# Zero matmuls in TensorE's waits and three loads spread out, at the head of a fused attention and FFN kernel

## The chip, the cores and the metric

The kernel runs on one core of a Trainium2 chip. The metric is the device time in microseconds (us) of one execution, taken as the median of several runs. The five engines of the core work side by side, each through its own queue in order: TensorE (PE in the profile, with its weight loads as PEld), VectorE (DVE), ScalarE (ACT), GpSimd (POOL) and SyncE (SP), which here issues most of the DMA transfers.

## The reference, cut to what matters

One transformer block on x of 2048 rows and 1024 columns in bf16: 32 heads of 32 columns that share one K and one V, and a gated FFN of 3584 columns.

```
h  = x + A(layernorm(x))
h2 = h + B(layernorm(h))

A(x): q = x @ wq              (32 heads of 32)
      k = x @ wk; v = x @ wv  (one head, shared)
      p = softmax(q k^T / sqrt(32))
      return (p v) @ wo
B(x): return (sigmoid(x @ w_gate) * (x @ w_up)) @ w_down
```

## The kernel before

**Units of work.** The rows of x are 16 tiles of 128. The attention runs in *bursts*: a burst is eight (later four) score matmuls on TensorE (`s_burst`, line 706, matmuls at 725 and 715) and two exponentials of 128x1024 on ScalarE (`one_exp`, line 748). The scores have six PSUM banks, and burst k waits on TensorE until all exponentials but one of the bursts before it are done. All other matmuls fill the time between bursts: projections, PV, the output projection and the FFN. They run as *groups* (`_Group`, `run_group`, `run_item`), each in one of the two banks of `X_ps`, and each ends with an eviction on VectorE or ScalarE. Groups of the kind "f" are those that go through `mm_list`, with the matmul of line 327.

**The head.** Up to the 25th burst the order is written out by hand (lines 1412 to 1532), with the strings of `HEAD` for the pieces between bursts. Layernorm of a tile is `ln1_stats` (VectorE, line 411, with GpSimd for the power), `ln1_sub` and `ln1_mult`. The tile is then transposed to `xnT`: tiles 0 and 1 on TensorE, tiles 2 to 15 by a DMA transpose that SP issues (`transposed`, line 533). Groups in the head:
- u0 to u7: a query projection for one of the first eight units of the attention, 16 matmuls of 128 columns; u7 and u4 read the last quarter of wq.
- K0 to K7: the keys of two tiles, 8 matmuls of 256 columns, evicted by ScalarE at line 556. K1 needs tiles 2 and 3, K2 tiles 4 and 5, K3 tiles 6 and 7.
- V0 to V7: the values of two tiles, 16 matmuls of 32 columns.

The order around the change is: burst 2, burst 3, u5, K1, burst 4, V1 and u6, burst 5, burst 6, K2, burst 7, V2, u7, u4, burst 8, a projection of 8 matmuls of 256 columns, burst 9, K3, V3. ScalarE's order is written out too: the eviction of K1 stands between the two exponentials of burst 3, that of K2 between those of burst 6, and that of K3 between those of burst 9.

**The planner.** While the program is written, the kernel keeps a clock of its own for each engine (`k_pe`, `k_act`, `k_dve`, `k_sp`, and `k_dma` for the transfers) and adds a written duration for each instruction. `when(...)` is the latest of the times at which ticks of semaphores fall by these clocks, plus 0.05; `need(engine, ...)` moves the engine's clock there and emits the waits. `mode(...)` adds 0.104 where TensorE changes the kind of its matmuls. A DMA transpose takes 1.3 of SP's clock, then 1.2 of the transfers' clock, and lands 2.0 later; a load takes its size by 275 KB per us of the transfers' clock, and lands 2.2 later. In the head the clocks do not choose an order. In the main loop (from line 1561) they do: a burst goes out when its due time has come by `k_pe`, otherwise a group's next item.

**Loads.** x comes in tiles of 256 KB. Tiles 0 to 7 are issued at the start. The others are issued by `ln1_out` (line 449) on SP's queue behind the transpose of the tile that `LOADS` names, as is "q3", the last quarter of wq, 512 KB.

**Zeros.** `zeros` (line 462) runs matmuls of 128 columns on an operand of zeros, whose result nobody reads: 64 at the start, 8 between the transposes of tiles 0 and 1, and 4 at some places of `HEAD` ("z").

Of the kernel before, what the change touches and what calls it, by code (L numbers as in the profile page):

```python
# [12 lines left out]
P = 128  # L13
# [39 lines left out]
def when(*ticks):  # L53

    return max([0.0] + [t[0].time(t[1]) + 0.05 for t in ticks if t is not None])


def need(eng, *ticks):
    clk = CLK[id(eng)]
    for t in ticks:  # L60
        if t is not None and t[0].emit is not None and t[1] > t[0].n:
            t[0].emit(t[1])
    clk[0] = max(clk[0], when(*ticks))
    for t in ticks:
        if t is not None:
            t[0].wait(eng, t[1])
# [18 lines left out]
def bass_sequential_preLN__grouped_kv_mqa__glu_gated_glu__prompt_kernel(  # L85
# [37 lines left out]
    G_SUM, NPB = 3, 4  # L123
    HG = 3
    HEAD = ['u', 'Vu', 'L', '', 'VULu', 'u', 'VPP', 'wL', 'LzPULz', 'zPLz', 'W', 'LzP', 'PPzL', 'VVL', 'PPV', '', 'UPP', 'UP', 'PV', 'U', 'PU', '', '', '']
    HEAD_U = [5, 6, 7, 4]
    ORDER = [(0, 0), (0, 1), (0, 2), (1, 0), (0, 3), (1, 1), (1, 2), (1, 3)]
    ORDER += [(t_, i_) for t_ in range(2, NT) for i_ in range(NQ // 2)]
# [10 lines left out]
    with ExitStack() as es:  # L139
# [31 lines left out]
        X_ps = EC(nc.psum_tensor("X_ps", [P, 2, 512], F32))  # L171

        k_pe, k_dve, k_act, k_pool, k_sp, k_dma = [0.0], [0.0], [0.0], [0.0], [0.0], [0.0]
# [4 lines left out]
        def ctr(name, clk=None):  # L178
            return _Ctr(EC(nc.semaphore(name)), clk)

        c_pe, c_dve, c_act = ctr("c_pe", k_pe), ctr("c_dve", k_dve), ctr("c_act", k_act)
        c_pool, c_s, c_e, c_pv = ctr("c_pool", k_pool), ctr("c_s", k_pe), ctr("c_e", k_act), ctr("c_pv", k_pe)
# [29 lines left out]
        def xn(t):  # L212
            return xn2[:, t % 4, :] if t % 4 < 2 else hn[:, t % 4 - 2, :]
# [25 lines left out]
        def _(unused):  # L239
            sp, pe, act, dve, pool = nc.sync, nc.tensor, nc.scalar, nc.vector, nc.gpsimd  # L240
# [34 lines left out]
            warm = pairs[:, 1, 0:256]  # L275
# [11 lines left out]
            bank_free = [None, None]  # L287
            pe_mode = [None]

            def mode(m):  # L290
                if pe_mode[0] != m:
                    k_pe[0] += T_SW
                    pe_mode[0] = m

            def bank_time(b):
                f = bank_free[b]
                return 1e9 if f == "open" else f(False) if callable(f) else when(f)

            def open_group(g):
                b = min((bank_time(b), b) for b in range(2) if bank_free[b] != "open")[1]  # L300
                g.bank = b
                f = bank_free[b]
                need(pe, f(True) if callable(f) else f)
                bank_free[b] = "open"

            main = [False]
# [5 lines left out]
            def by_columns(g):  # L312
                if not main[0]:
                    return False
                while issued and issued[0] < k_pe[0] - I_US:
                    issued.popleft()
                if 4 * len(issued) > I_MAX and g.items[0][0] < 0.2:
                    return False
                more = busy(pv[0]) or pv_follow[0] is not None
                if pe_mode[0] == "pv":  # L320
                    return more or k[0] < NB
                n = pv_next[0]
                return pe_mode[0] == "s" and (more or n < NQC * NQ and k[0] >= min(BPG * (n + 1) + 1, NB - (n == NQC * NQ - 1)))

            def mm(out, lhsT, rhs, start, stop):
# [4 lines left out]
                                    stop=stop, tile_position=(0, DH * j), skip_group_check=True)  # L330
                return ins

            def run_item(g):
                if g.bank is None:
                    need(pe, *[v() if callable(v) else v for v in g.after])
                    open_group(g)
                mode("pv" if g.kind == "f" and by_columns(g) else g.kind)
                issued.extend([k_pe[0]] * (2 if pe_mode[0] == "pv" else 0))
                part[0] = (part[0] + 1) % 2 if pe_mode[0] != "pv" else part[0]
                issued.extend([k_pe[0]] * (pe_mode[0] != "pv" and part[0]))  # L340
                fn = g.items.popleft()[1]
                tick = fn(X_ps[:, g.bank, :])
                if not g.items:
                    dve_fill(when(tick) + g.room)
                    bank_free[g.bank] = g.evac(X_ps[:, g.bank, :], tick)
# [56 lines left out]
            st_val, rs_val, nm_val = {}, {}, {}  # L402
            NSUB = 2
            mean_val, xc_val = {}, {}
            LOADS = {3: (8, 9, 10, 11), 5: ("q3",), 7: (12, 13), 9: (14,), 11: (15,)}

            def ln1_stats(t, parts=(0, 1)):
                slot = t % 4
# [37 lines left out]
            def xnT_tile(t):  # L446
                return xnT[:, t // TPQ, :, (t % TPQ) * P:(t % TPQ + 1) * P]

            def ln1_out(t):
                xnT_read[t] = xnT_val[t] = transposed(sp, xnT_tile(t), xn(t), t % 4, xn_val[t])  # L450
                for i in LOADS.get(t, ()):
                    if i == "q3":
# [77 lines left out]
            def transposed(eng, dst, src, slot, *ticks):  # L530
                need(eng, *ticks)
                c, clk = d_t[slot], CLK[id(eng)]
                eng.dma_start_transpose(dst, src).then_inc(c.sem, 16)
                c.n += 16
                clk[0] += 1.3
                if eng is sp:
                    k_dma[0] = max(clk[0], k_dma[0]) + 1.2
                c.at[c.n] = max(clk[0], k_dma[0] if eng is sp else 0.0) + 2.0
                return (c, c.n)

            k_val, v_val, q_val = {}, {}, {}
# [30 lines left out]
            def wide(g):  # L572
                return g >= NQ

            def key_tile(g, b):
                return ORDER[g][1] % 2 * BPG + b
# [70 lines left out]
            k = [0]  # L647
# [5 lines left out]
            def burst(k):  # L653
                if k <= HG:
                    return 0, k, 0
                if k < NH:
                    return 0, (k - HG - 1) % HG, 1 + (k - HG - 1) // HG
                return k // WSL, (k // BPG) % NQ, k % BPG

            def quad(k):  # L660
                return burst(k)[0] * NQ + burst(k)[1]
# [44 lines left out]
            def s_burst(k):  # L706
                g, b = quad(k), burst(k)[2]
                t, i = ORDER[g]
                mode("s")
                need(pe, (c_e, 2 * k - 1) if k > 0 else None, k_val[key_tile(g, b) // 2 if wide(g) else b],  # L710
                     *q_ready(g), *(xnT_ready(0, 1) if k < 2 else ()))
                if wide(g):
                    kt = key_tile(g, b)
                    for j in range(4):
                        ins = pe.matmul(S_ps[:, ((2 * k + j // 2) % 3) * 2 + j % 2, :],  # L715
                                        lhsT=kT4[DH * j:DH * (j + 1), kt * P:(kt + 1) * P],
                                        rhs=QT[DH * j:DH * (j + 1), i // 2 * 4:i // 2 * 4 + 4, t * P:(t + 1) * P],
                                        start=True, stop=True, tile_position=(DH * j, 0))
                        if j % 2 == 1:
                            c_s.inc(ins, 0.113, 0.3)  # L720
                    return
                for kt in range(2):
                    for j in range(4):
                        bank = ((2 * k + j // 2) % 3) * 2 + j % 2
                        ins = pe.matmul(S_ps[:, bank, kt * QC:(kt + 1) * QC],
                                        lhsT=kT4[DH * j:DH * (j + 1), (2 * b + kt) * P:(2 * b + kt + 1) * P],
                                        rhs=QT[DH * j:DH * (j + 1), 2 * i:2 * i + 2, t * P:(t + 1) * P],
                                        start=True, stop=True, tile_position=(DH * j, 0))
                        if kt == 1 and j % 2 == 1:
                            c_s.inc(ins, 0.115, 0.3)  # L730
# [319 lines left out]
            def dve_fill(until):  # L1050

                while True:
                    held = set()
                    for i, (chain, cost, fn, ready) in enumerate(lo):
                        if chain in held:
                            continue
                        t = ready()
                        if t is not None and max(t, k_dve[0]) + cost <= until:
                            break
                        held.add(chain)  # L1060
                    else:
                        return
                    lo.pop(i)
                    fn()
# [364 lines left out]
            xnT_val[1] = [pe_out(act, 1, 0, 1, f0), pe_out(dve, 1, 1, 2, f1)]  # L1429
            u_list = collections.deque([("u", g) for g in HEAD_U] + [("q", q) for q in range(NQ)])  # L1430

# [12 lines left out]
            def head(i, p):  # L1444
                for x in HEAD[i]:
                    if x == "V":
# [253 lines left out]
```

## Time and profile before

| | us |
|---|---|
| median of three runs | 1099.19 |
| the three runs | 1098.35, 1099.19, 1100.61 |
| the profiled execution, its time | 1100.04 |
| its span, from the first to the last instruction | 1098.0 |
| TensorE busy (matmuls) | 1078.1 |
| ScalarE busy | 1007.3 |
| VectorE busy | 897.7 |

In the profile's rows a time is counted from the span's start. A timeline row gives the start, the duration until the last of its instructions ended, the engine, the line, the operation, what it writes and reads, how many instructions were merged (x...), and in brackets how long the engine was idle before and what ended that. The rows of DMA issues give a transfer's tile, the queue that issued it, its size, and the time from the issue to the landing. In a table of stretches, PEclk is the granted TensorE clock as a share of full speed.

### The profile page before, as it was taken

The numbers are of one execution on the slowest core, as the hardware profiler recorded it, in microseconds if no ns is written. First come the engines' busy times: TensorE is split into PE (matmuls) and PEld (weight loads), VectorE is DVE, ScalarE is ACT, GpSimd is POOL, SyncE is SP. The second block draws the span as 40 slices with busy tenths as digits, with TensorE's granted clock in tenths as the row PEclk, the third lists the DMA queues.
The fourth block names the chain that finished last, engine by engine and source line by source line (L and its number), as shares of the span: only waits on it lengthen the run. The fifth ranks groups of instructions, "written<-read, shape, count | busy, mean of one in ns | idle before, by whom it ended". The sixth has DMA issues, their size and how long they took to land. (4 is left out here: it accounts for less than half of the span.)

```text
span 1098.0 us, 33628 instructions
## 1 busy us (share of the span) xinstructions
PE 1078.1 (98%) x14725; PEld 628.5 (57%) x14725; DVE 897.7 (82%) x1494; ACT 1007.3 (92%) x1155; POOL 65.4 (6%) x136
## 2 busy tenths in 40 slices
PE   6899999999999999999999999999999999999999
PEld 5564456643666446653666447653666447653884
DVE  7759997799988989799989899898898899798311
ACT  6899999999999999999999999999999999999110
POOL 4500110010000000000000000000000000000000
PEclk9899999999999999999999999999999999999999
DMA  9743428850976539780997709770698509872570
GB/s 219 141 99 109 126 53 245 244 159 21 232 206 187 143 83 256 203 211 25 225 245 201 173 24 269 200 184 25 143 274 224 121 26 274 221 191 79 145 181 20
DMA packets 332418, 175.84 MB, mean 160 GB/s; under 512 B 39536, under 2 KB 326512, under 8 KB 332272
## 3 DMA queue, kind: packets, MB, share of 16 engines
q1 hardware_dynamic: 326464, 163.47, 58.8%
q0 software_dynamic: 2544, 9.44, 2.6%
q8 instruction: 116, 1.90, 0.8%
q10 hardware_dynamic: 3264, 0.79, 0.4%
q14 instruction: 30, 0.25, 0.1%
HBM read 161.61 MB, written 4.19 MB: 151 GB/s over the span
## 5 line engine op out<-in xcount | busy, mean ns | idle before, releaser
L748 ACT ACTIVATE Pr<-S_ps 128x1024 bf16<-128x1024 f32 x992 | 943.9, 1206 | 4.7 <-PE S_ps L715 3.0
L798 DVE TENSOR_TENSOR pairs<-Pr 128x1024 bf16<-128x1024 bf16 x446 | 303.9, 684 | 28.4 <-ACT Pr L748 27.6
L810 DVE TENSOR_TENSOR pairs<-pairs 128x1024 bf16<-128x1024 bf16 x390 | 269.0, 690 | 11.4
L327 PE MATMUL X_ps<-QT,wgu 128*128 128x128 bf16 (+1 forms) x2263 | 209.4, 243 | 2.0 <-DMA wgu<-in_B_w_up_dram 2.0
L327 PEld LDWEIGHTS X_ps<-QT,wgu 128*128 128x128 bf16 x2263 | 163.8, 98 | 40.3 <-issue 28.2
L715 PE MATMUL S_ps<-QT,kT 32*128 32x512 bf16 x1792 | 177.0, 385 | 1.4 <-ACT Pr L748 0.9
L327 PE MATMUL X_ps<-zone,hact 128*128 128x512 bf16 (+2 forms) x686 | 157.5, 372 | 0.0
L327 PE MATMUL X_ps<-QT 128*128 128x128 bf16 (+1 forms) x1652 | 153.0, 242 | 0.3 <-DMA QT<-in_B_w_gate_dram 0.3
L327 PEld LDWEIGHTS X_ps<-QT 128*128 128x128 bf16 x1652 | 119.8, 98 | 26.0 <-issue 16.0
L1231 ACT ACTIVATE gu<-X_ps 128x512 f32<-128x512 f32 x112 | 87.1, 777 | 45.7 <-PE X_ps L327 45.6
L715 PEld LDWEIGHTS S_ps<-QT,kT 32*128 32x128 bf16 x1792 | 45.3, 91 | 134.9 <-ACT Pr L748 123.2
L1252 DVE SCALAR_TENSOR_TENSOR hact<-gu,X_ps 128x512 bf16<-128x512 f32 x112 | 76.6, 684 | 49.7 <-PE X_ps L327 48.5
L872 PE MATMUL X_ps<-Pr,V 128*32 128x512 bf16 x1792 | 114.9, 381 | 0.4
L327 PEld LDWEIGHTS X_ps<-zone,hact 128*128 128x128 bf16 x686 | 59.1, 98 | 74.0 <-issue 18.5
L872 PEld LDWEIGHTS X_ps<-Pr,V 128*32 128x32 bf16 x1792 | 41.6, 96 | 48.3 <-issue 13.8
L327 PE MATMUL X_ps<-zone 128*128 128x512 bf16 (+3 forms) x506 | 62.3, 272 | 2.7 <-DMA zone<-zone 1.2
L329 PE MATMUL X_ps<-zone,hact 128*32 128x512 bf16 x952 | 61.3, 380 | 0.0
L379 POOL CAST mean<-mv 128x1 f32<-128x1 bf16 x28 | 8.8, 316 | 818.1 <-DVE mv L1123 803.7
L327 PE MATMUL X_ps<-wo,QT 128*128 128x512 bf16 x232 | 57.1, 381 | 0.0
L329 PE MATMUL X_ps<-QT,wgu 128*32 128x256 bf16 (+1 forms) x1636 | 50.9, 264 | 0.0
L327 PEld LDWEIGHTS X_ps<-zone 128*128 128x128 bf16 x506 | 34.3, 101 | 24.9 <-issue 7.9
L329 PEld LDWEIGHTS X_ps<-QT,wgu 128*32 128x32 bf16 x1636 | 39.0, 97 | 11.2 <-issue 6.6
(106 smaller groups left out, 708.9 us busy)
## 6 DMA issues: line engine op xcount, KB each, us to landing
wgu<-in_B_w_up_dram SPq DMA_DIRECT2D x81, 512.0 KB, 5.6
wgu<-in_B_w_gate_dram SPq DMA_DIRECT2D x72, 512.0 KB, 5.6
QT<-in_B_w_gate_dram SPq DMA_DIRECT2D x57, 512.0 KB, 5.7
QT<-in_B_w_up_dram SPq DMA_DIRECT2D x48, 512.0 KB, 6.7
zone<-in_B_w_down_dram POOLq DMA_DIRECT2D x14, 512.0 KB, 5.9
out_dram<-hx SPq DMA_DIRECT2D x31, 128.0 KB, 1.7
hx<-in_A_x_dram SPq DMA_DIRECT2D x15, 256.0 KB, 3.1
Pr<-in_B_w_gate_dram SPq DMA_DIRECT2D x5, 512.0 KB, 7.1
```

Source lines behind the costliest of these rows:

```text
L327: return pe.matmul(out, lhsT=lhsT, rhs=rhs, start=start, stop=stop, skip_group_check=main[0])
L329: ins = pe.matmul(out[DH * j:DH * (j + 1)], lhsT=lhsT[:, DH * j:DH * (j + 1)], rhs=rhs, start=start, stop=stop, tile_position=(0, DH * j), ...
L379: return c_pool.inc(pool.tensor_copy(out=mean[:, i:i + 1], in_=mv[:, i:i + 1, 0]), 0.2)
L715: ins = pe.matmul(S_ps[:, ((2 * k + j // 2) % 3) * 2 + j % 2, :], lhsT=kT4[DH * j:DH * (j + 1), kt * P:(kt + 1) * P], rhs=QT[DH * j:DH * ( ...
L748: c_e.inc(act.activation(out=p_tile(k, n % 2), in_=S_ps[:, 2 * pr:2 * pr + 2, :].rearrange("p a (b q) -> p (a b) q", q=QC), func=ACTF.Exp, ...
L798: slot_use[x] = c_dve.inc(dve.tensor_tensor(out=dst(x), in0=p_tile(k - 1, hh), in1=p_tile(k, hh), op=ALU.add), T_ADD, 0.08)
L810: slot_use[x] = slot_use[y] = c_dve.inc(dve.tensor_tensor(out=pairs[:, x, :], in0=pairs[:, x, :], in1=pairs[:, y, :], op=ALU.add), T_ADD, ...
L872: ins = pe.matmul(bank[DH * j:DH * (j + 1), :], lhsT=V[:, kt, :], rhs=p_tile(k, j // 2)[:, j % 2 * 2:j % 2 * 2 + 2, :], start=b == 0, stop ...
L1231: tanh_val[n] = c_act.inc(act.activation(out=slot, in_=bank, func=ACTF.Tanh, scale=0.5), T_TANH, 0.1)
L1252: gu_read[n] = c_dve.inc(dve.scalar_tensor_tensor(out=hact[:, 2 * fs[0]:2 * fs[0] + ft, r0:r0 + len(ts) * P], in0=slot.rearrange("p (a b) ...
```

## The change

Two edits. First, a new function `keep_busy` puts zero matmuls into TensorE's queue ahead of a wait. It is called in `run_item` ahead of the waits of every group of kind "f" that has no bank yet, as long as the head lasts (`main[0]` is false), and in `s_burst` for bursts 1 to 9, there for the exponentials and the keys and not for the queries. It takes the bank of `X_ps` that the planner's clock has free first, waits for it, and runs as many zeros at 0.058 each as fit by that clock between now (or the bank's time) and the due time, less a margin of 0.15, or 0.35 where TensorE last ran another kind; fewer than three are left out. Second, tiles 9, 10 and 11 of x, which were issued with tile 8 behind the transpose of tile 3, are issued one by one behind the transposes of tiles 4, 5 and 6; the last quarter of wq keeps its place behind tile 5 and is now followed by tile 10.

```diff
+    K_BUSY = 10
...
+            def keep_busy(*ticks):
+                free = sorted((bank_time(b), b) for b in range(2) if bank_free[b] is not None and bank_free[b] != "open")
+                if main[0] or not free:
+                    return
+                n = int((when(*ticks) - max(k_pe[0], free[0][0]) - (0.15 if pe_mode[0] == "f" else 0.35)) / 0.058)
+                if n < 3:
+                    return
+                b = free[0][1]
+                f = bank_free[b]
+                need(pe, f(True) if callable(f) else f)
+                mode("f")
+                for i in range(n):
+                    pe.matmul(X_ps[:, b, 0:P], lhsT=warm[:, 0:P], rhs=warm[:, 0:P], start=True, stop=True,
+                              skip_group_check=True)
+                    k_pe[0] += 0.058
+
             def run_item(g):
                 if g.bank is None:
-                    need(pe, *[v() if callable(v) else v for v in g.after])
+                    after = [v() if callable(v) else v for v in g.after]
+                    if g.kind == "f":
+                        keep_busy(*after)
+                    need(pe, *after)
                     open_group(g)
...
-            LOADS = {3: (8, 9, 10, 11), 5: ("q3",), 7: (12, 13), 9: (14,), 11: (15,)}
+            LOADS = {3: (8,), 4: (9,), 5: ("q3", 10), 6: (11,), 7: (12, 13), 9: (14,), 11: (15,)}
...
             def s_burst(k):
                 g, b = quad(k), burst(k)[2]
                 t, i = ORDER[g]
+                if 0 < k < K_BUSY:
+                    keep_busy((c_e, 2 * k - 1), k_val[b])
                 mode("s")
```

## The prediction

> **What bounds the kernel now.** I read the page's busy shares and slices first, then the clock in stretches, then the timeline of the stretch that stands out.
>
> ```profile
> span 1098.0 us, 33628 instructions
> ...
> ACT  6899999999999999999999999999999999999110
> ...
> PEclk9899999999999999999999999999999999999999
> ...
> L748 ACT ACTIVATE Pr<-S_ps 128x1024 bf16<-128x1024 f32 x992 | 943.9, 1206 | 4.7 <-PE S_ps L715 3.0
> ```
>
> From the third slice to the 37th ScalarE is full, and its 992 exponentials of line 748 wait 4.7 us in all: the attention is a chain of exponentials, and the FFN tail follows it on TensorE in a fixed order. Only the head, before about 50 us, has holes, and only there (second slice) is the granted clock below full. So whatever time the exponentials gain or lose in the head should move everything behind them, both engines alike, to the end.
>
> ```profile
> 14.90:18.30 3.40, 2.12 (x48) 1.63 (x48) 2.96 (x9) 2.47 (x3) 1.23 (x2) 1.00 0.72 91
> 21.70:25.10 3.40, 2.12 (x48) 1.51 (x48) 3.16 (x8) 3.40 (x5) 1.65 (x5) 1.00 1.18 187
> 25.10:28.50 3.40, 1.43 (x16) 0.83 (x16) 3.19 (x9) 2.47 (x4) 2.70 (x8) 1.00 1.03 231
> 28.50:31.90 3.40, 2.45 (x37) 1.97 (x38) 2.24 (x6) 2.87 (x4) 2.71 (x6) 0.50 1.33 200
> 31.90:35.30 3.40, 3.40 (x34) 2.61 (x33) 2.70 (x6) 0.90 (x2) 0.39 (x1) 0.50 0.54 164
> ```
>
> The columns are the stretch, its length, the busy time of PE, PEld, DVE, ACT and POOL, the clock, the DMA share and GB/s. The clock is half from 28.5 to 35.3 us, 6.8 us long, behind a stretch in which TensorE was busy for 1.43 of 3.40 us. Stretches with 2.12 of 3.40 busy kept it. The timeline shows what it costs:
>
> ```profile
> 25.53 0.40 PE L725 MATMUL S_ps<-QT,kT 32*128 32x256 bf16 x8 [1.71 <-ACT Pr L748]
> 26.21 1.10 ACT L748 ACTIVATE wo<-S_ps 128x1024 bf16<-128x1024 f32 x1
> 27.16 1.03 PE L327 MATMUL X_ps<-zone 128*128 128x256 bf16 x8 [1.24 <-DMA zone<-zone]
> 28.23 0.38 ACT L556 ACTIVATE kT<-X_ps 128x256 bf16<-128x256 f32 x1 [0.93 <-PE X_ps L327]
> 28.76 0.61 PE L725 MATMUL S_ps<-QT,kT 32*128 32x256 bf16 x8 [0.56 <-ACT kT L556]
> 29.31 0.61 PE L327 MATMUL X_ps<-zone 128*128 128x32 bf16 x16
> 29.42 1.95 ACT L748 ACTIVATE hact<-S_ps 128x1024 bf16<-128x1024 f32 x2
> 30.61 3.60 PE L327 MATMUL X_ps<-zone 128*128 128x128 bf16 x32 [0.69 <-DMA zone<-in_A_wq_dram]
> 34.13 0.61 PE L725 MATMUL S_ps<-QT,kT 32*128 32x256 bf16 x8
> 34.24 0.38 ACT L612 ACTIVATE QT<-X_ps 128x256 bf16<-128x256 f32 x1 [2.87 <-PE X_ps L327]
> 34.78 1.94 ACT L748 ACTIVATE Pr<-S_ps 128x1024 bf16<-128x1024 f32 x2 [0.16 <-PE S_ps L725]
> ```
>
> Burst 6 (25.53) and K2 (27.16) stand behind waits of 1.71 and 1.24 us, the second for the transposes of tiles 4 and 5; the clock then falls, and u7 and u4 (30.61, 32 matmuls) take 3.60 us. ScalarE is idle for 2.87 us until 34.24. The first exponential of burst 8, at 34.78, is my marker: ScalarE stays full behind it.
>
> **The zeros: what one costs, and whether they keep the clock.**
>
> ```profile
> 8.13 0.61 PE L467 MATMUL X_ps<-pairs 128*128 128x128 bf16 x8
> 12.63 1.74 PE L327 MATMUL X_ps<-zone 128*128 128x128 bf16 x28
> ```
>
> At full clock 28 matmuls of 128 columns take 1.74 us and 8 zeros 0.61, so 20 more are 1.13: 0.0565 us each, where the planner books 0.058. In the new order the emptiest 3.4 us, about 24.8 to 28.2, hold ten zeros ahead of burst 6 (0.56), burst 6 (0.40), twelve ahead of K2 (0.68) and 0.56 of K2: 2.2 us, just over the 2.12 that kept the clock and far over the 1.43 that lost it. So I take it that the clock stays full; if not, see the rivals.
>
> **Where the zeros delay real work.** They are in TensorE's own queue, so what stands behind them waits until the last has run. Their number comes from the kernel's own clock, not from the wait. That clock books a transpose with 1.3 + 1.2 + 2.0 = 4.5 us from its issue to its landing.
>
> ```profile
> zone<-hn SPq DMA_TRANSPOSE x1, 3.1
> ...
> 18.74 0.40 PE L725 MATMUL S_ps<-QT,kT 32*128 32x256 bf16 x8 [1.22 <-ACT wo L748]
> 19.07 2.04 PE L327 MATMUL X_ps<-zone 128*128 128x128 bf16 x24
> ...
> 21.15 0.38 ACT L556 ACTIVATE kT<-X_ps 128x256 bf16<-128x256 f32 x1 [0.35 <-PE X_ps L327]
> 21.68 0.40 PE L725 MATMUL S_ps<-QT,kT 32*128 32x256 bf16 x8 [0.56 <-ACT kT L556]
> 22.01 1.47 PE L327 MATMUL X_ps<-zone 128*128 128x32 bf16 x32
> ```
>
> - Burst 3 (18.74): the gap of 1.22 us gets 17 zeros by the planner's due time, 0.96 us; they begin 0.33 behind the burst before (as 22.01 stands to 21.68) and fit. Cost 0, bounds 0 and 0.1.
> - K1 (the last 8 of the 24 matmuls at 19.07): tile 3's transpose landed 3.1 us after its issue, not 4.5, so u5 and K1 run on end to end, with no wait in the row. The planner believes in a wait of 4.5 − 3.1 = 1.4 us; by its clock it is 1.3, and after the margin of 0.15 that makes 20 zeros, 1.1 us. This is real delay of K1, of its eviction (21.15) and of burst 4. Bounds 0.9 and 1.2.
> - Burst 4 (wait 0.56): 9 zeros, 0.5 us, they fit. Behind it ScalarE has no idle time (3.40 of 3.40 busy from 21.7 to 25.1), so the 1.1 us arrive whole at burst 6: 25.53 + 1.1 = 26.63. Its 10 zeros first wait for u6's eviction on ScalarE, and only burst 6, which waits longer, stands behind them: cost 0.
> - K2: the planner books tile 5's transpose behind the load of x tile 9 and sees 1.05 us to go; less 0.35, 12 zeros, 0.68 us. K2 starts at 26.63 + 0.33 + 0.68 = 27.64, 0.48 later than before. Its transposes have landed by then (below).
> - Burst 7 gets 9 zeros inside its wait of 0.56, burst 9 and K3 about 3 each, 0.2 us, where ScalarE still has an exponential in hand: 0, bounds 0 and 0.3.
>
> **The loads.** The moved issues stay on SP's queue.
>
> ```profile
> 18.22 2.01 SPq L243 DMA_DIRECT2D wgu<-in_A_x_dram  x4
> 22.95 2.13 SPq L533 DMA_TRANSPOSE zone<-zone  x1
> 25.12 0.58 SPq L243 DMA_DIRECT2D zone<-in_A_wq_dram  x1
> ...
> zone<-zone SPq DMA_TRANSPOSE x1, 4.1
> zone<-in_A_wq_dram SPq DMA_DIRECT2D x1, 512.0 KB, 5.4
> zone<-hn SPq DMA_TRANSPOSE x1, 3.5
> ...
> 28.50 1.28 DVE L411 BATCH_NORM_STATS2 st<-wgu 128x6 f32<-128x512 bf16 x2
> 33.79 1.28 DVE L411 BATCH_NORM_STATS2 st<-wgu 128x6 f32<-128x512 bf16 x2
> 36.29 1.44 PE L327 MATMUL X_ps<-zone 128*128 128x256 bf16 x24
> ```
>
> Four issues took 2.01 us, 0.5 each. Tile 5's transpose (issued 22.95, landed 4.1 later, 27.05) now stands behind the issue of tile 9: up to 0.35 us later by the queue, up to 1.0 earlier if it lands after 3.1 as tile 3's did. Either way it is there before 27.64: worth nothing here, because the zeros last longer than the wait did. The last quarter of wq landed at 25.12 + 5.4 = 30.5, which u7 waited for. With 0.5 MB less ahead of it, and the issue of 2.13 us nearer to tile 2's and 3's 1.24, I expect it 0.3 to 1.2 us earlier, 29.3 to 30.2; with no gain 30.5. Tiles 9 and 10 are first read at 28.50 and 33.79, over 4 us after their new issues: hidden. What is later is tile 7's transpose, now behind tiles 10 and 11: K3 (36.29) needs it. It landed at 28.62 + 3.5 = 32.1, and 0.5 MB at the 200 to 231 GB/s of those stretches is 2.2 to 2.6 us, partly offset by the earlier queue: 33 to 34.7.
>
> **The sum.** K2 27.64, its eviction 28.23 + 0.48 = 28.71 (ScalarE is free at 26.21 + 1.10 + 1.1 = 28.41), burst 7 29.24. V2 follows 0.33 later at full clock and takes 0.57 (the row at 22.01 is such a group and 16 matmuls of 128 columns: 1.47 − 0.90): u7 at 30.14, and I take the weights as there. u7 and u4 at full clock are 1.74 + 4 × 0.0565 = 1.97 instead of 3.60, and burst 8 starts, as before, 0.08 ahead of their modelled end: 32.03. The exponential came 0.65 behind burst 8; less 0.1 for the clock, 32.57. Against 34.78 that is **2.2 us** earlier. Bounds: weights as late as before, 1.8; K1's zeros at 0.9 and the weights early, 2.5. K3 is then wanted 2.2 us earlier, at 34.1, with 0.5 us of ScalarE work in hand: just covered if tile 7 lands by 34.6.
>
> The profiled execution took 1100.04 us (span 1098.0 and 2.04 around it): 1097.8 on its own scale. It is 0.85 above the median of the three runs; I hold that for scatter common to both kernels, so on the median's scale 1099.19 − 2.2 = **1097.0**. 0.2%, about what a measurement of this kernel can tell from no change, is also 2.2 us: the forecast stands on that line.
>
> **The rivals.**
> - *The cold stretch is not in the median run* (chance 0.08). The three runs lie 2.3 us apart, as much as the cold stretch costs. Had the clock stayed full, u7 and u4 would have ended 1.63 earlier and the marker stood at about 33.0; the change would bring 0.5: 1098.7. The Trainium skill (TensorE: Matmul & The Clock Gate, "What's actually happening") says that the activity window is free-running, so its phase differs from run to run, and that the clock halves after an idle window of 3.4 us; here a window that was 42% busy (1.43 of 3.40) was enough, so the row decides on that point. The half-clock length of 6.8 us, two such windows, agrees.
> - *The clock falls all the same* (0.05). If it halves at 28.5 as before, u7 and u4 take 3.60 again from 30.14 on, the marker stands near 34.4, and nine half-speed zeros ahead of burst 7 add 0.4: 34.8, no gain, 1099.2.
> - *The moved loads make K3 wait* (0.09). If tile 7 lands at 35.6, K3 and the exponentials behind it lose 1.0: 1098.0. For it: the 0.5 MB now ahead of it; against: the DMA share fell to 0.54 in the stretch up to 35.3.
> - *K1's zeros cost less than I hold* (0.11), as when tile 3 lands later than in this execution: then up to 1.1 less at K1, after which the wq quarter sets u7, at 29.7: marker 32.1 or a little earlier, gain 2.7 to 3.2, 1096.2.
> - *The main loop's order changes for the worse* (0.17). The planner decides between a burst and a filling group by its own clock, which is 0.5 us later from K2 on; if its engines' clocks don't all move alike, groups stand ahead of bursts.
>
> ```profile
> 38.93 1.90 PE L327 MATMUL X_ps<-zone 128*128 128x512 bf16 x8
> ```
>
> One group of 512 columns ahead of a burst is up to 1.90 us without an exponential. From two such places on (3.8 against 2.2) the kernel is slower; three make 1099.2 − 2.2 + 5.7 = 1102.7. For it: only 4.7 us of waits in line 748, so any new one shows. Against: the bursts in the planner's second half of the head are due by the exponentials, so its clocks should move together.
>
> **How the numbers follow.** The forecast holds 0.50, within 1096.4 and 1097.9. Its middle lies on the line; the bound of 1.8 needs moved loads that bring the weights no earlier, which the long issue at 22.95 speaks against, so I put 0.33 of it on faster and 0.17 on the same. Faster: 0.33, 0.11 of K1's rival, and 0.02 for an order that happens to be better, 0.46. The same: 0.17 + 0.08 + 0.05 + 0.09 = 0.39. Slower: 0.15 of the last rival. The range for 8 in 10 leaves out most of that 0.15 and a little below: 1095.2 to 1100.0.
>
> **What would show it.** No half clock in the head; 20 zeros ahead of K1 and its eviction at 22.2; burst 6 near 26.6, K2 near 27.6 with no DMA wait, u7 near 30.1; 32 matmuls in about 2 us; the marker near 32.6, and the same distance from there to the end. I am wrong if the clock falls all the same, if K1's eviction stays near 21.15, if K3 waits for a DMA, or if line 748 waits for clearly more than 4.7 us.

## The result and the profile after

| | before | changed | ratio, 95% interval |
|---|---|---|---|
| median, us | 1099.19 (7 runs) | 1095.98 (7 runs, 1094.68 to 1097.57) | 0.9976 [0.9966, 0.9986] |
| the same two kernels, compared again | 1098.76 (35 runs) | 1096.57 (11 runs) | 0.998 [0.9971, 0.9989] |
| profiled execution: time, span | 1100.04, 1098.0 | 1095.99, 1094.1 | |

The changed kernel is faster, by 3.2 us in the first comparison and by 2.2 in the second, 0.2 to 0.3% with both intervals below 1. The predicted 1097.0 is 1.0 us above the first median, inside the range.

The page of the changed kernel:

```profile
span 1094.1 us, 33732 instructions
...
ACT  6999999999999999999999999999999999999110
...
PEclk9999999999999999999999999999999999999999
...
L770 ACT ACTIVATE Pr<-S_ps 128x1024 bf16<-128x1024 f32 x992 | 943.6, 1204 | 3.2 <-PE S_ps L747 1.4
```

The one slice below full clock is gone, ScalarE's second slice went from 8 to 9, and the exponentials wait 3.2 us instead of 4.7. Their busy time is what it was (943.6 against 943.9). The clock in stretches, with the columns explained ahead of the prediction's second fence:

```profile
21.70:25.10 3.40, 3.34 (x65) 2.60 (x62) 3.16 (x8) 2.58 (x4) 1.73 (x5) 1.00 0.79 156
25.10:28.50 3.40, 2.36 (x39) 1.84 (x36) 3.19 (x9) 3.40 (x5) 2.70 (x8) 1.00 1.11 282
28.50:31.90 3.40, 3.34 (x68) 2.95 (x66) 2.69 (x8) 3.09 (x5) 2.71 (x6) 1.00 1.52 221
```

Where TensorE was busy for 1.43 us between 25.1 and 28.5 it is now busy for 2.36, and the stretch behind it runs at 1.00 instead of 0.50. The timeline of the head, in the order of time (L346 are the zeros, whose numbers stand at the row's end):

```profile
17.38 1.12 PE L346 MATMUL X_ps<-pairs 128*128 128x128 bf16 x17
19.90 1.28 PE L346 MATMUL X_ps<-pairs 128*128 128x128 bf16 x20
21.45 1.03 PE L328 MATMUL X_ps<-zone 128*128 128x256 bf16 x8 [0.27 <-DMA zone<-hn]
22.52 0.38 ACT L576 ACTIVATE kT<-X_ps 128x256 bf16<-128x256 f32 x1 [1.80 <-PE X_ps L328]
26.90 0.40 PE L747 MATMUL S_ps<-QT,kT 32*128 32x256 bf16 x8 [0.24 <-ACT Pr L770]
27.23 0.84 PE L346 MATMUL X_ps<-pairs 128*128 128x128 bf16 x12
27.91 1.04 PE L328 MATMUL X_ps<-zone 128*128 128x256 bf16 x8
28.98 0.38 ACT L576 ACTIVATE kT<-X_ps 128x256 bf16<-128x256 f32 x1 [0.31 <-PE X_ps L328]
29.84 2.36 PE L328 MATMUL X_ps<-zone 128*128 128x32 bf16 x48
32.14 0.40 PE L747 MATMUL S_ps<-QT,kT 32*128 32x256 bf16 x8
32.57 1.94 ACT L770 ACTIVATE Pr<-S_ps 128x1024 bf16<-128x1024 f32 x2
33.98 1.44 PE L328 MATMUL X_ps<-zone 128*128 128x256 bf16 x24
```

The marker stands at 32.57, where it was predicted, against 34.78 before: 2.21 us. ScalarE's hole ahead of K2's eviction shrank from 0.93 to 0.31, and the hole of 2.87 us ahead of the second query eviction is gone, since V2, u7 and u4 (29.84, 48 matmuls) take 2.36 us instead of the 0.61 + 3.60 with a wait between them. One row is not as predicted. K1 (21.45) stood behind a DMA at the last: its 20 zeros ended at 21.18, and it waited 0.27 us more. The DMA views of stretches show which (transfers with the time from issue to landing, and q8, the queue that loads TensorE's instructions, with packets, MB and share; in the kernel before it carries 116 loads of 16 KB, one for every 254 of TensorE's 29,450 matmuls and weight loads):

```profile
q8 instruction: 1, 0.02, 3.9%
...
zone<-hn SPq DMA_TRANSPOSE x1, 4.5
...
zone<-zone SPq DMA_TRANSPOSE x1, 3.1
...
zone<-in_A_wq_dram SPq DMA_DIRECT2D x1, 512.0 KB, 4.5
...
zone<-hn SPq DMA_TRANSPOSE x1, 5.3
```

They are, from the top: an instruction load of 0.02 MB between 18.5 and 20.0, then the transposes of tiles 3 and 4, the last quarter of wq, and tile 7's transpose. Tile 3's took 4.5 us where it had taken 3.1, with the instruction load in the middle of it. Before, that stretch had no such load, and one came between 20.5 and 22.0.

The profiled pair differs by 3.90 us in span: 2.21 up to the marker and 1.7 in the main loop behind it. The instructions stand in the same order there on every engine, so the 1.7 come from waits: a standstill of TensorE that cost ScalarE 0.45 us near 174 and that the changed kernel doesn't have (below); waits for FFN weights, 2.02 us in two places before and 1.18 in one after; and about 0.4 in small pieces.

### The profile page after: what moved, and what is told of

It reads as the page before. It is cut to its first block, busy times and chain, and to the rows that moved or that the text cites. A ratio compares the mean times of both kernels' runs of the same rounds, so it can differ in the third digit from the quotient of the medians.

```text
span 1094.1 us, 33732 instructions
## 1 busy us (share of the span) xinstructions
PE 1075.0 (98%) x14751; PEld 632.2 (58%) x14804; DVE 897.4 (82%) x1494; ACT 1007.0 (92%) x1155; POOL 65.8 (6%) x136
## 5 line engine op out<-in xcount | busy, mean ns | idle before, releaser
L770 ACT ACTIVATE Pr<-S_ps 128x1024 bf16<-128x1024 f32 x992 | 943.6, 1204 | 3.2 <-PE S_ps L747 1.4
L328 PE MATMUL X_ps<-zone,hact 128*128 128x512 bf16 (+2 forms) x652 | 150.0, 371 | 4.4 <-issue 3.8
L328 PEld LDWEIGHTS X_ps<-zone,hact 128*128 128x128 bf16 x686 | 59.2, 98 | 73.9 <-issue 18.5
L328 PE MATMUL X_ps<-wo,QT 128*128 128x512 bf16 x213 | 53.7, 380 | 1.4 <-issue 0.6
```

Of the source, the lines that this page charges most:

```text
L328: return pe.matmul(out, lhsT=lhsT, rhs=rhs, start=start, stop=stop, skip_group_check=main[0])
L770: c_e.inc(act.activation(out=p_tile(k, n % 2), in_=S_ps[:, 2 * pr:2 * pr + 2, :].rearrange("p a (b q) -> p (a b) q", q=QC), func=ACTF.Exp, ...
```

## The experiments

They ran in three groups, each on one chip beside the unchanged kernel: the first four, the next four, the last three. All times are medians in us; n is the number of runs.

| run | time (n) | before beside it (n) | ratio, 95% interval | marker |
|---|---|---|---|---|
| e1_before_again | 1097.27 (1) | 1098.32 (29) | | 33.30 |
| e1_zeros_only | 1096.20 (12) | 1098.32 (29) | 0.9973 [0.9963, 0.9984] | 32.61 |
| e1_loads_only | 1098.61 (12) | 1098.32 (29) | 1.0 [0.9989, 1.001] | 34.73 |
| e1_no_k1_zeros | 1096.78 (12) | 1098.32 (29) | 0.9982 [0.9972, 0.9992] | 32.52 |
| e2_after_again | 1096.57 (11) | 1098.76 (35) | 0.998 [0.9971, 0.9989] | 32.91 |
| e2_from_burst4 | 1097.59 (11) | 1098.76 (35) | 0.999 [0.9979, 1.0001] | 32.08 |
| e2_shift8 | 1098.27 (11) | 1098.76 (35) | 0.9995 [0.9987, 1.0004] | 32.35 |
| e2_shift14 | 1098.18 (12) | 1098.76 (35) | 0.9993 [0.9983, 1.0004] | 33.95 |
| e3_pad | 1096.54 (6) | 1099.65 (17) | 0.9971 [0.9959, 0.9982] | 32.50 |
| e3_no_s3_zeros | 1097.96 (10) | 1099.65 (17) | 0.9985 [0.9975, 0.9995] | 32.28 |
| e3_best | 1096.63 (6) | 1099.65 (17) | 0.9966 [0.9954, 0.9978] | 32.45 |

### How long is the clock half in an execution of before?

The kernel before, unchanged, one more profile.

> The kernel before, unchanged, for a second trace of it. Theory: the half clock in the head belongs to the kernel and not to one execution, so it comes again, 6.8 us long, starting between 25 and 30 us, and the first exponential of burst 8 (the marker) stands between 33.6 and 35.5 us. The loop behind the head holds waits for the FFN weights that differ from run to run by up to 2 us. Rival: the clock stays full in some executions; then the marker stands near 33.0.

Its stretches:

```profile
25.30:28.70 3.40, 1.60 (x24) 0.98 (x24) 3.19 (x9) 2.57 (x5) 2.70 (x8) 1.00 1.19 270
28.80:32.10 3.30, 2.90 (x44) 2.65 (x38) 1.96 (x6) 2.33 (x3) 2.60 (x6) 0.50 1.02 188
32.20:35.50 3.30, 3.17 (x45) 2.20 (x43) 2.40 (x6) 2.52 (x5) 0.68 (x3) 1.00 0.60 154
```

A stretch with 1.60 us of TensorE lost the clock as well, but here it was half for one stretch (28.71 to 32.12) and not two, and the marker came at 33.30. So the head's gain is 2.2 us against one execution and 0.7 against another. The mean granted clock over the whole span, which each run has, tells which is the usual one: 3.4 us at half clock are 0.16% of 1098 us, so one stretch gives 0.998, two give 0.997 and three 0.995. Of the 81 executions of before in the three groups:

| mean clock | executions of before | median, group of 29 | median, group of 35 | executions of the changed kernel |
|---|---|---|---|---|
| 1.000 | 0 | | | 18 |
| 0.998 | 11 | 1097.41 | 1097.54 | 0 |
| 0.997 | 65 | 1098.68 | 1098.77 | 0 |
| 0.995 | 5 | 1102.03 | 1102.36 | 0 |

The clock falls in each of these 81 executions of before and in none of the changed kernel (7 runs in its first comparison, 11 in the second). By these medians an execution with a second cold stretch is 1.2 to 1.3 us longer. One with a third is another 3.3 to 3.6 us longer, more than the 1.7 us that half a clock can take from 3.41 us of matmuls, so those five lost something else too; none of them has a profile. Two are usual: the profiled execution was typical.

### The two parts of the change, each alone

Zeros alone:

```diff
-            LOADS = {3: (8,), 4: (9,), 5: ("q3", 10), 6: (11,), 7: (12, 13), 9: (14,), 11: (15,)}
+            LOADS = {3: (8, 9, 10, 11), 5: ("q3",), 7: (12, 13), 9: (14,), 11: (15,)}
```

> The zeros alone, the loads as before. Theory: the clock stays full; K1 is 1.1 us late as in the changed kernel; ahead of K2 only 3 zeros are written instead of 12, because the planner books tile 5's transpose 0.5 us earlier; u7 waits for the last quarter of wq, which lands near 30.5; marker near 33.0, 1.8 us before the old one: 1097.4 at the median, if the loop behind the head moves with the marker. Rival (the loads carry the gain): no faster than before, 1099.2.

The loads alone are the kernel before with the changed kernel's `LOADS`.

> The loads alone, no zeros in the waits. Theory: K1 is not delayed, K2 starts near 26.7, the last quarter of wq lands near 29, and u7 starts near 29.4, but the clock falls and u7 and u4 take 3.6 us: marker near 33.6, 1.2 us gained, 1098.0. Rival (the earlier transposes shorten the waits enough that the clock holds): marker near 31.9, 1096.3 or less, faster than the changed kernel.

The zeros carry the whole gain (0.9973), with the clock at 1.000 in all 12 runs and the marker at 32.61. From their timeline:

```profile
30.29 1.96 PE L328 MATMUL X_ps<-zone 128*128 128x128 bf16 x32 [0.22 <-DMA zone<-in_A_wq_dram]
32.61 1.94 ACT L770 ACTIVATE Pr<-S_ps 128x1024 bf16<-128x1024 f32 x2
```

The weights landed late here (30.24 instead of 28.91), and u7 waited 0.22 us for them. But only 3 zeros stood ahead of K2, not 12, so V2 started at 29.50 instead of 29.84, and u7 began at 30.29, where it began at 30.26 in the changed kernel.

The moved loads alone do nothing (1.0). In the kernel with the loads alone the stretches are:

```profile
23.50:26.90 3.40, 0.86 (x19) 0.24 (x16) 3.19 (x9) 3.40 (x6) 2.59 (x8) 1.00 1.07 165
27.00:30.40 3.40, 2.06 (x13) 1.18 (x16) 3.29 (x9) 1.17 (x3) 2.34 (x6) 0.50 1.34 282
```

and its timeline at K2 and at the marker:

```profile
27.78 1.87 PE L327 MATMUL X_ps<-zone 128*128 128x256 bf16 x8 [1.70 <-issue]
34.73 1.02 ACT L748 ACTIVATE Pr<-S_ps 128x1024 bf16<-128x1024 f32 x1
```

Tile 5's transpose landed at 27.69, not earlier than before (27.07), so the marker of 33.6 that was expected did not come: K2 waited 1.70 us, a stretch went by with 0.86 us of TensorE, and K2 itself ran at half clock (1.87 instead of 1.03). The clock was half from 26.96 to 33.79, again two stretches.

### What held K1: its zeros or tile 3's transpose?

The changed kernel without the 20 zeros ahead of K1:

```diff
-                    if g.kind == "f":
+                    if g.kind == "f" and not g.quiet:
                         keep_busy(*after)
...
-                return _Group(items, evac, [wk4_val] + xnT_ready(2 * p, 2 * p + 1))
+                g = _Group(items, evac, [wk4_val] + xnT_ready(2 * p, 2 * p + 1))
+                g.quiet = p == 1
+                return g
```

> The changed kernel without the 20 zeros ahead of K1. Theory: they are pure delay, 1.1 us of K1 and of every exponential behind it, so K1's eviction stands near 21.15 again, burst 6 near 25.6, K2 near 26.7, marker near 31.4: 1.1 us less than the changed kernel, 1094.9. Rival (they keep the clock full): without them the clock falls, u7 and u4 take 3.6 us, marker 33 or later, 1096.5 or more.

Its timeline:

```profile
21.40 1.03 PE L329 MATMUL X_ps<-zone 128*128 128x256 bf16 x8 [1.38 <-issue]
22.47 0.38 ACT L577 ACTIVATE kT<-X_ps 128x256 bf16<-128x256 f32 x1 [1.79 <-PE X_ps L329]
...
175.66 0.83 PE L331 MATMUL X_ps<-QT,wgu 128*32 128x256 bf16 x23 [1.45 <-issue]
176.43 0.60 ACT L1256 ACTIVATE gu<-X_ps 128x512 f32<-128x512 f32 x1 [0.94 <-PE X_ps L331]
```

Neither theory expected this: the clock held in 11 of 12 runs, and K1's eviction was still late. With no zeros there K1 still starts at 21.40, after 1.38 us of nothing: tile 3's transpose landed at 21.31. And the kernel lost time elsewhere, 1.45 us in the middle of a run of FFN matmuls that have nothing to wait for. Two new questions followed: why tile 3 is late, and what the standstill near 175 is.

### Why tile 3's transpose is late

The theory: the 17 zeros ahead of burst 3 bring TensorE to the end of its loaded instructions earlier, the next load of 16 KB then runs while tile 3's transpose is in flight, and the transpose is held up by it. The rival: the transpose varies by itself, or is slowed by the zeros or the other loads. Four kernels on one chip: the changed kernel again; the same without the zeros ahead of bursts 1 to 3 and of K1; and that with 8 or 14 zeros ahead of burst 1, in a scores bank that is free, to move the instruction load back.

> The changed kernel once more, for a second trace and for times beside the three that follow. Theory F (TensorE's own instruction fetch, a 16 KB transfer, holds up a DMA transpose that is in flight, and the 17 zeros ahead of burst 3 bring that fetch forward onto tile 3's): the fetch comes near 19.0 again, tile 3's transpose lands near 21.3, K1's eviction stands near 22.5, tile 4's lands in about 3 us, marker near 32.5, 1096.0. Rival G (tile 3's late landing in the traces with zeros is chance): it lands near 20.0, K1 begins at 21.1 behind its zeros.

```diff
-                if 0 < k < K_BUSY:
+                if 3 < k < K_BUSY:
```

(with the edit of K1's zeros from above)

> The changed kernel without the zeros ahead of burst 3 and ahead of K1; all later zeros stay. F: the fetch comes at 21 or later as in the kernel before, tile 3's transpose lands near 20.0 and K1's eviction is back at 21.2, but tile 4's transpose lands near 26.1 and tile 5's near 27.7 as with the loads alone, so K2 starts near 27.8 and the marker stands near 32.3: the same time as the changed kernel, 1095.8. Rival H (the delay at K1 is the zeros' own): K1 at 21.2 and everything behind it 1.0 us earlier, marker 31.5, 1095.0.

```diff
+                if k == 1:
+                    for _ in range(8):
+                        pe.matmul(S_ps[:, 4, 0:P], lhsT=warm[:, 0:P], rhs=warm[:, 0:P], start=True, stop=True)
```

> As e2_from_burst4, with 8 zeros ahead of burst 1, which wait for nothing and end inside that burst's wait: they only move the place in TensorE's instruction stream. F: the fetch comes between 19.5 and 20.5, behind tile 3's transfer and ahead of tile 4's, both land in about 3.1 us; K1's eviction near 21.2, K2 near 26.7, marker near 31.5, 1.0 us less than the changed kernel, 1095.0. Rival (the place in the instruction stream doesn't matter): the same as e2_from_burst4.

The same with 14:

> As e2_shift8, with 14 zeros ahead of burst 1, nearly the number of instructions that the changed kernel has ahead of K1's transpose. F: the fetch is back near 19.2, tile 3's transpose lands near 21.3 and K1's eviction at 22.4, though nothing stands between u5 and K1; marker near 32.4, 1096.0. Rival (the place in the instruction stream doesn't matter): K1's eviction near 21.2.

With 8 zeros the instruction load did not move (21.09, against 21.06 without them), so that run decides nothing about the theory. With 14 it came at 19.73, and the DMA views of that kernel show

```profile
q8 instruction: 1, 0.02, 3.9%
...
zone<-hn SPq DMA_TRANSPOSE x1, 4.9
```

in the stretches 18.5 to 20.0 and 17.0 to 18.1: tile 3's transpose is late, with no zeros ahead of burst 3 at all. Over all profiles of this study (starts of the instruction load, and times from tile 3's issue to its landing, from the traces):

| instruction load | kernels | tile 3's transpose |
|---|---|---|
| 18.85 to 19.73, between the end of its issue (near 18.1) and its landing | changed, the same again, zeros alone, no K1 zeros, 14 zeros, e3_pad | 4.43 to 4.86 |
| 21.06 or later | before, the same again, loads alone, from burst 4, 8 zeros, e3_no_s3_zeros, e3_best | 3.04 to 3.06 |

Six against seven, with no overlap, and the position of the load was moved on purpose in both directions. Tile 11's transpose, where no edit was aimed, says the same: 4.77 and 4.81 in the two profiles in which a load began between the end of its issue and its landing (loads alone at 46.64, before again at 45.29), 3.03 to 3.11 in the other eleven. I take the collision as shown; how the load delays the transpose is not visible. A load in the last 0.3 us before the landing cost nothing (tile 14 in the changed kernel: load at 52.23, landed 52.49, 3.05). What one does that runs during the issue differs from tile to tile and stays open. Tile 4's transpose (issued near 21.2) fits: 3.04 to 3.06 in the nine profiles (eight kernels) that have the x tiles spread out and no instruction load after the transpose's issue had ended; 4.68 with the loads alone, where one came at 23.69; 4.18 with the zeros alone, where four x tiles were queued ahead; 4.88 and 4.90 in the two profiles of before, which have the four x tiles and an instruction load at 21.10 or 22.83. So the moved loads did make tile 4's transpose faster. Nothing waited for it.

The timeline of the kernel with zeros from burst 4 on shows what K1's delay had covered:

```profile
21.01 0.38 ACT L577 ACTIVATE kT<-X_ps 128x256 bf16<-128x256 f32 x1 [0.34 <-PE X_ps L329]
32.08 1.94 ACT L773 ACTIVATE Pr<-S_ps 128x1024 bf16<-128x1024 f32 x2
34.35 1.43 PE L329 MATMUL X_ps<-zone 128*128 128x256 bf16 x24 [0.80 <-DMA zone<-hn]
...
176.06 0.42 PE L331 MATMUL X_ps<-QT,wgu 128*32 128x256 bf16 x7 [1.02 <-issue]
```

K1's eviction is at 21.01 and the marker at 32.08, 0.5 earlier than in the changed kernel. Then K3 stands 0.80 us for tile 7's transpose (landed 34.22), and 1.02 us are lost near 176. The kernel with 8 zeros goes the same way: marker at 32.35, then K3 waits 1.03 us and 0.61 is lost near 176. Both had been expected as fast as the changed kernel or faster (1095.8 and 1095.0) and came out slower than it, at 1097.59 and 1098.27: an earlier marker was worth nothing there. With 14 zeros ahead of burst 1 K1 waited with nothing in the wait:

```profile
21.86 1.86 PE L329 MATMUL X_ps<-zone 128*128 128x256 bf16 x8 [1.75 <-issue]
23.76 0.38 ACT L577 ACTIVATE kT<-X_ps 128x256 bf16<-128x256 f32 x1 [2.99 <-PE X_ps L329]
```

It lost the clock for 21.34 to 24.75 in this profile and in part of its runs (mean clock under 1.000 in 6 of 12). So a late tile 3 puts the clock at risk. In the kernels whose profiles show tile 3 late, the clock was lost in 6 of 12 runs with no zeros ahead of burst 3 and K1 (14 zeros), in 1 of 18 with those ahead of burst 3 alone (e1_no_k1_zeros, e3_pad), and in none of 30 with both (the changed kernel twice, the zeros alone).

### What K1's zeros cost when tile 3 is on time

The changed kernel without the zeros ahead of burst 3 (`if 3 < k < K_BUSY`), but with those ahead of K1.

> The changed kernel without the 17 zeros ahead of burst 3; the 20 ahead of K1 stay. This prices K1's zeros alone. The prediction's step (20 zeros are 1.1 us of real delay where tile 3's transpose has landed at 20): K1 begins at 21.1, its eviction stands at 22.2, marker near 32.5, ratio 0.998. Rival (K1's zeros cost nothing by themselves): the eviction at 21.2, or, if the fetch still meets tile 3's transpose, at 22.5 with the transpose landing at 21.3.

Its timeline:

```profile
20.04 1.28 PE L346 MATMUL X_ps<-pairs 128*128 128x128 bf16 x20
21.16 1.04 PE L328 MATMUL X_ps<-zone 128*128 128x256 bf16 x8
22.23 0.38 ACT L576 ACTIVATE kT<-X_ps 128x256 bf16<-128x256 f32 x1 [1.37 <-PE X_ps L328]
```

Tile 3 had landed at 20.06, and the zeros alone hold K1. From burst 3's start (18.81) to K1's eviction it is 3.42 us, where before it was 21.15 − 18.74 = 2.41: the 20 zeros cost 1.01. The kernel is no faster for a marker at 32.28: K3 waited 1.03 for tile 7 (landed 34.66), and 1.41 went near 176.

### The standstill near 175

The kernel before has it too; its timeline there:

```profile
173.14 0.29 PE L327 MATMUL X_ps<-QT,zone 128*128 128x128 bf16 x2 [0.32 <-issue]
174.84 1.94 ACT L748 ACTIVATE Pr<-S_ps 128x1024 bf16<-128x1024 f32 x2 [0.45 <-PE S_ps L715]
```

TensorE stands still for 0.32 us with nothing to wait for. Theory: it depends on how many TensorE instructions stand ahead. Rival: it comes from the times of the head. The kernel without K1's zeros gets its 20 zeros back at other bursts, so that 79 zeros stand ahead as in the changed kernel:

```diff
+    PAD = {15: 6, 18: 4, 19: 10}
...
+                if k in PAD:
+                    need(pe, (c_e, 2 * k - 2))
+                    for _ in range(PAD[k]):
+                        pe.matmul(S_ps[:, 2 * k % 3 * 2, 0:P], lhsT=warm[:, 0:P], rhs=warm[:, 0:P], start=True, stop=True,
+                                  skip_group_check=True)
                 mode("s")
```

> e1_no_k1_zeros, with 20 zeros put into three later waits of the head (6 ahead of burst 15, 4 ahead of burst 18, 10 ahead of burst 19), so that TensorE's instruction stream behind the head is as long again as the changed kernel's. Theory I (where an instruction fetch falls in the loop decides whether TensorE stands still in the dense run of column matmuls near 175 us): the still time of 1.45 us there, which the four kernels without K1's zeros all have in some size, is gone, as in the changed kernel; 0.8 us less than e1_no_k1_zeros by the ratio to before, 0.9975. Rival (that still time is chance, or belongs to the missing zeros themselves): it stays, and the ratio with it at 0.9982 or above.

Its timeline:

```profile
174.12 1.38 PE L332 MATMUL X_ps<-QT,wgu 128*32 128x256 bf16 x43 [0.16 <-issue]
175.75 1.82 PE L332 MATMUL X_ps<-QT,wgu 128*32 128x256 bf16 x60
```

The 1.45 us are down to 0.16. The marker stands at 32.50, as without the padding (32.52), so the head's times are not what changed. Each row below is one or more profiles: the added zeros ahead of this place, the standstill, and the time from the start of the last TensorE instruction load to the standstill's end.

| added zeros | kernels | standstill | load's start to its end |
|---|---|---|---|
| 0 | before, the same again, loads alone | 0.32, 0.18, 0.32 | 2.58, 2.62, 2.49 |
| 42 | from burst 4 | 1.02 | 2.50 |
| 50, 56 | 8 zeros, 14 zeros | 0.61, 1.11 | 2.49, 2.57 |
| 59, 62 | no K1 zeros, e3_no_s3_zeros | 1.45, 1.41 | 2.57, 2.56 |
| 68, 70 | e3_best, zeros alone | none | |
| 79 | changed, the same again, e3_pad | none, none, 0.16 | 2.56 (e3_pad) |

In all nine the standstill ends 2.49 to 2.62 us after a load has begun, whatever its length. The reading that fits is that TensorE has used up its loaded instructions and stands until the next ones are there; no view shows its store of instructions, so this part is argued. How many zeros stand ahead goes far to decide whether that point falls among these matmuls: putting the 20 back took away all but 0.16 us with the head's times unchanged. It isn't all, since the same 79 gave none twice and 0.16 once.

### A version from what was learned

No zeros ahead of bursts 1 to 3 and K1, tiles 10 to 13 issued one transpose later so that tile 7 lands in time, and padding:

```diff
+    PAD = {6: 4, 15: 6, 18: 4, 19: 12}
...
-            LOADS = {3: (8,), 4: (9,), 5: ("q3", 10), 6: (11,), 7: (12, 13), 9: (14,), 11: (15,)}
+            LOADS = {3: (8,), 4: (9,), 5: ("q3",), 6: (10,), 7: (11, 12, 13), 9: (14,), 11: (15,)}
```

> e2_from_burst4 with x tile 10 behind tile 6's and tile 11 behind tile 7's transpose, so that one load less stands ahead of tile 7's, and with 26 zeros in later waits (4 at burst 6, 6 at 15, 4 at 18, 12 at 19). Theory: K1's eviction near 21.1, marker near 32.1 as there, K3 no longer waits for tile 7 (lands near 33.2), no still time near 175: 0.7 us less than the changed kernel, ratio 0.9972. Rival (the next late transfer takes the place of K3's): marker or K3 later by what was won, ratio 0.998.

```profile
21.39 0.38 ACT L578 ACTIVATE kT<-X_ps 128x256 bf16<-128x256 f32 x1 [0.35 <-PE X_ps L330]
32.45 1.94 ACT L779 ACTIVATE Pr<-S_ps 128x1024 bf16<-128x1024 f32 x2
33.85 1.44 PE L330 MATMUL X_ps<-zone 128*128 128x256 bf16 x24
```

K3 no longer waits (tile 7 landed at 33.60), and nothing is lost near 175. The ratio, 0.9966, is the lowest of the study, but its interval overlaps the changed kernel's and e3_pad's: it beats the kernel before and isn't told apart from the others.

## Why the prediction was right, point by point

**The bound and the marker: right.** The marker at 32.57 was met to the hundredth, 2.21 us of gain, which is partly luck (below), and the zeros ahead of burst 3, K1, burst 4, K2 and burst 7 numbered 17, 20, 9, 12 and 9 as worked out (9 instead of 10 ahead of burst 6, and none ahead of K3). That a gain in the head travels to the end is borne out: the second comparison shows 2.2 us between the medians.

**Clock kept: right.** 18 of 18 executions at 1.000. The stretch that had to carry it holds 2.36 us of TensorE, where 2.2 were predicted. The prediction's bound, between 1.43 and 2.12, can be drawn closer. In the second profile of before the last change of the clock lies 1092.26 us behind the first, 320 steps of 3.413 us. Cut into such steps from its first change of the clock, each of the ten profiles that show one gives the same picture. The steps at full clock with 0.82, 1.40, 1.43 and 1.61 us of TensorE (the row of before again above gives 1.60, for a stretch 0.01 shorter) were followed by half clock. All others kept it, the lowest with 1.80, 1.83, 1.91 and 1.95: the bound lies between 1.61 and 1.80, about half. At half clock 2.03 and 2.47 us did not bring the full clock back, and 2.90 and 3.01 did. This accounts for the varying length of the drop: the first cold step held 2.47 us in the first profile of before and 3.01 in the second.

**Cold stretch not in the median run: fell.** The median execution of before has two cold stretches, as the profiled one. What the rival had right is that the length varies: 11 of 81 had only one. Against those the gain was about 1.0 us (1097.54 − 1096.57), where the rival had 0.5. The Trainium skill (TensorE: Matmul & The Clock Gate, "What's actually happening") calls the activity window free-running, 3.4 us long; half-clock times of 3.41 and 6.83 us in one program agree. That the clock halves after an idle window does not describe these runs: windows with 1.43 and 1.60 us of matmuls were followed by half clock.

**K1's zeros: the price was right, the place of the wait was not.** The step took tile 3's transpose at 3.1 us from the profile of before and made the 20 zeros the only delay. Their price was predicted at 1.1 and measured at 1.01, in the kernel where tile 3 is on time. In the changed kernel itself the delay is 22.52 − 21.15 = 1.37, and the last part of it is the transpose, which the other zeros had pushed to 4.5 us by way of the instruction load. The rival that K1's zeros cost less because tile 3 lands later had the condition and missed the consequence: K1 is then late anyway. The missing row in the prediction was that of the instruction queue.

**From burst 6 to burst 8: each 0.1 to 0.3 late, the sum right by an offset.** Burst 6 was at 26.90 (predicted 26.63), K2 at 27.91 (27.64), burst 8 at 32.14 (32.03): K1's 1.37 instead of 1.1 runs through. It comes out again because V2, u7 and u4 took 2.36 us and not 0.57 + 1.97 = 2.54, and because the exponential stood 0.43 behind burst 8 rather than 0.54. That two small errors cancel a third to the hundredth is luck; that each is under 0.3 us is not.

**The loads: tile 5 worth nothing, right; the weights worth up to 0.4, wrong.** The last quarter of wq took 4.5 us instead of 5.4 and landed at 28.91, a little ahead of the expected band, and u7 did not wait for it. But the bound of 1.8 for late weights did not hold: with the zeros alone they landed at 30.24, and the marker's gain was still 2.17. There the planner wrote 9 zeros fewer ahead of K2, which won back what the weights cost. In time the zeros alone aren't told apart from both parts.

**K3: right, but with 0.16 us to spare.** Tile 7's transpose landed at 33.82 (33 to 34.7 predicted), and K3 started at 33.98. In three runs with an earlier marker and the same loads (from burst 4, 8 zeros, e3_no_s3_zeros; 32.08 to 32.35) the rival came true: K3 waited 0.80 to 1.03 us. At a marker of 32.50 (e3_pad) it still waited 0.28.

**The main loop's order: the rival fell.** The order is the same on all engines.

**Left over: 1.0 us.** The medians of the first comparison are 1.0 us further apart than the sum. Of the 1.7 us that the profiled pair gained behind the marker, 0.45 is the standstill near 174 that the new instruction count removes. The waits for FFN weights are scatter as far as seen: 2.02 and 1.17 us in the two profiles of before, 1.18 and 1.41 in those of the changed kernel, 0.26 and 0.41 in those of the zeros and of the loads alone. How much of the 1.0 is lasting stays open; the second comparison shows none of it.

## What to carry to other kernels

Zeros in a wait pay where a stretch of 3.4 us would otherwise hold too few matmuls (here under half of it), and they cost nothing only if the wait is real: check the planner's durations against the trace at each place. Every added instruction also moves the later instruction loads and whatever they collide with, so an added no-op is not neutral even where the engine is idle. When a wait in the middle of a head goes away, look at the next transfer's landing against the new start, here 0.16 us, before counting the gain.

## What had not been expected of the hardware

- An instruction load of 16 KB for TensorE that begins behind the issue of a DMA transpose and well ahead of its landing: 4.43 to 4.86 us from issue to landing, against 3.04 to 3.06.
- TensorE standing still for 0.16 to 1.45 us in a run of matmuls that wait for nothing, until 2.49 to 2.62 us after an instruction load has begun, in some numbers of instructions ahead and not in others.
- Half clock comes in whole pieces of 3.41 us, one, two or three of them by the mean clock, in executions of one and the same program. It follows a stretch with 1.61 us of matmuls or less, and none with 1.80 or more; matmuls on zeros count as others do.
